# Two decoder layers with their gradients on one core: operand rows of dW in four row strips, and the first dW2 work moved ahead of the attention loop

## The chip, the cores and the metric

The kernel runs on one core of a Trainium2 chip. The metric is the device time in microseconds of one execution; the time before is the median of 7 runs. TensorE (PE) does matmuls and transposes, VectorE (DVE) and ScalarE (ACT) do everything that reads PSUM, GpSimd (POOL) issues the stores to HBM and SyncE (SP) the loads from HBM.

## The reference

Two layers, each an attention block and an MLP, share their weights. One token for each of two sequences passes through them, and the kernel returns the output and the gradients with respect to x, both caches, and all weights and biases.

```python
def _A_ref(x, k_cache, v_cache, wq, wo):       # x [2,1,1024], caches [2,4,16384,128]
    q = (x @ wq).reshape(B, Sq, 32, 128).transpose(0, 2, 1, 3)
    k, v = jnp.repeat(k_cache, 8, axis=1), jnp.repeat(v_cache, 8, axis=1)
    p = _softmax(jnp.einsum("bhqd,bhkd->bhqk", q, k) * Dh ** -0.5)
    o = jnp.einsum("bhqk,bhkd->bhqd", p, v)
    return o.transpose(0, 2, 1, 3).reshape(B, Sq, 4096) @ wo
def _B_ref(x, w1, b1, w2, b2):                  # w1 [1024,3584], w2 [3584,1024]
    h = _gelu(jnp.einsum("bsd,df->bsf", _layernorm(x), w1) + b1)
    return jnp.einsum("bsf,fd->bsd", h, w2) + b2
...
x = x + _A_ref(_layernorm(x), k, v, wq, wo); x = x + _B_ref(_layernorm(x), w1, b1, w2, b2)   # twice
_out, _vjp = jax.vjp(_f, x, k_cache, v_cache, wq, wo, w1, b1, w2, b2)
return (_out, *_vjp(grad_out))
```

The gradients of the caches (out_2, out_3) are 33.6 MB each. Those of the weights (out_4 for wq, out_5 for wo, out_6 for w1, out_8 for w2) are sums of four outer products each: two layers by two sequences.

## The kernel before, in words

Forward and backward passes run layer by layer; each streams the weights or the caches through SBUF in tiles of 128 x 4096 bf16 (1.05 MB). A pool `ld` has seven such buffers. One tile of K or V is a chunk of 4096 positions of one of eight groups (sequence x KV head); four chunks make a group. Four K and four V tiles of the last group (`keepK0` to `keepV3`) and one of each of another group (`keepxK`, `keepxV`) stay in SBUF from the earlier layer.

The change lies in the last stage, the backward pass of attention in layer 0, in which all big gradients are also written:

- **The wo stage.** `wob = Ahead(A_wo, ...)` loads wo in eight chunks of four rows. For each row `row(j)` turns the weights with eight transposes (`turn`, L313), and four iterations later `products(j)` multiplies them with the gradient (L340) into the PSUM tile `dops`. The last four rows are turned in iterations 28 to 31.
- **delta.** `do_delta` makes from `dops` the scaled gradient `doT_bf` and its dot product with the attention output, a chain of one matmul (`part_sum`) and some ten small DVE instructions that ends in `dlr`.
- **Operand rows.** The outer products need their operands as four rows (layer x sequence) on partitions. `rows_unit` (L949) transposes columns of `h_all`, `dh_all`, `o_all`, `dq_all` (into `rowsA`) and `gM_all`, `m_all`, `gA_all`, `n_all` (into `rowsB`); each pair of operands has one strip of 32 partitions of its own: strip 0 for dW2, 1 for dW1, 2 for dWo, 3 for dWq.
- **Units.** A unit of `dw_units` is one matmul of 4 rows by 128 x 512 (L1018) and its cast to bf16 in an SBUF tile, on ACT or DVE (`evac_cast`, L156 and L159; `pick` takes the engine with the smaller charged load). Eight units fill a tile of dW2 (seven of dW1), and `store` hands it to POOL's queue. Such a tile is called a home. Units wait in `fill`, those of dWq in `late`.
- **The opening.** The four kept chunks of the last group are done first: `scores` (L1194), a matmul with `dlr` (L1198), the product with the probabilities (L1202, `ds0`), the pairs `kv_pair` that make dV (L1159, eight matmuls and four casts for each half), and `dq_quad` (L411).
- **The loop.** Each step m turns two quarters of a V chunk (L1304), computes their scores, runs pairs for dK and dV, and calls `step_fill` for one unit (m < 4) or five.

All instructions stand in the order in which the Python code emits them, and each engine's queue runs in that order. Which SBUF tile a load or a home takes is also fixed when the program is written: two deques hold the free tiles, `by_read` (last read by an engine) and `by_store` (last given to a store). `new_home` takes from `by_read` first, `load_tile` from `by_store` first, `pump` issues loads while enough tiles are free. A load into a tile from `by_store` waits in SP's queue until that store has landed.

In PSUM there are two banks for transposes (`tp`), four for general use (`x`), one for accumulation and one small one (`sm`).

Of the kernel before, what the change touches and what calls it, by code (L numbers as in the profile page):

```python
# [23 lines left out]
def kernel(  # L24
# [50 lines left out]
    NLD = 7  # L75
    WIDE = 32
# [60 lines left out]
    def charge(eng, us):  # L137
        load[eng] += us
# [37 lines left out]
    def part_sum(src, n, name):  # L176
        ps = pm_([128, n], F32, name)
        PE.matmul(ps[:], lhsT=onesf[:], rhs=src, start=True, stop=True)
        return ps
# [520 lines left out]
    n_all = vec.tile([128, DJ, 4], BF16, name="n_all")  # L700
    o_all = vec.tile([128, HQ, 4], BF16, name="o_all")
    dq_all = vec.tile([128, HQ, 4], BF16, name="dq_all")
    gA_all = vec.tile([128, DJ, 4], BF16, name="gA_all")
    m_all = vec.tile([128, DJ, 4], BF16, name="m_all")
    h_all = vec.tile([128, FJ, 4], BF16, name="h_all")
    dh_all = vec.tile([128, FJ, 4], BF16, name="dh_all")
    gM_all = vec.tile([128, DJ, 4], BF16, name="gM_all")
# [86 lines left out]
    def attn_out_bwd(l, gT):  # L794
        V.tensor_copy(out=gA_all[:, :, lsl(l)], in_=gT[:])
        _, dops = w_pass(A_wo, HD, D, "do_ps", gT_bf=gA_all[:, :, lsl(l)])
        return do_delta(l, dops)

    def do_delta(l, dops):
# [5 lines left out]
        doT_bf = vec.tile([128, G, 8], BF16, name=f"doT_bf{l}")  # L805
        V.tensor_copy(out=doT_bf[:], in_=dof[:])
        prod = wrk.tile([128, G, 8], F32, name="dprod")
        V.tensor_tensor(out=prod[:], in0=dof[:], in1=sv["oT"][:], op=ALU.mult)
        dlp = part_sum(prod[:].rearrange("p g r -> p (g r)"), G * 8, "dl_ps")
        rest_ = wrk.tile([128, G * 8], F32, name="dl_rest")  # L810
        V.tensor_scalar(out=rest_[:], in0=dlp[:], scalar1=-1.0, scalar2=None, op0=ALU.mult)
# [12 lines left out]
        saved[f"a{l}"]["doT_bf"] = doT_bf  # L824
        return doT_bf
# [98 lines left out]
    for j in range(wob.J + 4):  # L924
        some(rest, 1)
        if j >= wob.J - 4 and j < wob.J:
            wob.row(j)
        if j >= 4:
            wob.products(j - 4, dops, gA_all[:, :, lsl(0)])
    TP = [pt([128, 8, 128], BF16, "tpm%d" % i) for i in range(2)]  # L930
    for t in TP:
        V.memset(t[:].bitcast(F32), 0.0)
    do_delta(0, pairs(dops, HQ))

    rowsA = ld.tile([128, LDW], BF16, name="rowsA", tag="ld")
    rowsB = wrk.tile([128, D], BF16, name="rowsB", tag="rowout")

    def rows_unit(srcs, dst, j0):  # L940

        def u():
            tp = mtp()
            n = 0
            for i, (colT, jlo) in srcs.items():
                jn = min(8, colT.shape[1] - jlo)
                n = max(n, jn)
                for j in range(jn):
                    PE.transpose(tp[32 * i:32 * i + 4, j, :], colT[:, jlo + j, :], ident[:], tile_position=(0, 32 * i))  # L949
            lo, hi = 32 * min(srcs), 32 * max(srcs) + 4  # L950
            evac_bf16(dst[lo:hi, j0 * 128:(j0 + n) * 128], tp[lo:hi, 0:n, :].rearrange("p a b -> p (a b)"), n * 128)

        return Unit(u)

    X = [px([128, 512], F32, "xm%d" % i) for i in range(4)]
    rot = {"x": 0, "tp": 0}


    by_read = deque(ld.tile([128, LDW], BF16, name="big", tag="ld") for _ in range(NLD - 1))
    by_store = deque()  # L960

    def nxt(what, lst):
        rot[what] += 1
        return lst[(rot[what] - 1) % len(lst)]

    def mx():
        return nxt("x", X)

    def mtp():
        return nxt("tp", TP)  # L970

# [13 lines left out]
    class Unit:  # L985
        def __init__(self, f, home=False):
            self.f, self.home = f, home

        def ready(self):
            return not self.home or n_free() > 3  # L990
# [4 lines left out]
    def dbias(rows, i, n, out_ap, name):  # L995
        p = 32 * i
        row = new_home()
        for c0 in range(0, n, 512):
            ps = mx()
            PE.matmul(ps[p:p + 1, :], lhsT=ones_bf[p:p + 4, 0:1], rhs=rows[p:p + 4, c0:c0 + 512], start=True, stop=True,  # L1000
                      tile_position=(p, p))
            evac_cast(row[p:p + 1, c0:c0 + 512], ps[p:p + 1, :], 512)
        store(out_ap.rearrange("(o f) -> o f", o=1), row[p:p + 1, 0:n], row)

    def dw_units(xrows, yrows, i, chunks, y0, ny, out_of):

        p = 32 * i
        box = {}
        units = []
        for j0, rb in chunks:  # L1010
            for j in range(rb):
                for c0 in range(0, ny, 512):
                    def u(j0=j0, rb=rb, j=j, c0=c0):
                        if j == 0 and c0 == 0:
                            box["t"] = new_home()
                        sv_ = box["t"][:, 0:rb * ny].rearrange("p (j n) -> p j n", j=rb)
                        ps = mx()
                        PE.matmul(ps[:], lhsT=xrows[p:p + 4, (j0 + j) * 128:(j0 + j + 1) * 128],  # L1018
                                  rhs=yrows[p:p + 4, y0 + c0:y0 + c0 + 512], start=True, stop=True, tile_position=(p, 0))
                        evac_cast(sv_[:, j, c0:c0 + 512], ps[:], 512)  # L1020
                        if j == rb - 1 and c0 + 512 >= ny:
                            store(out_of(j0, rb), sv_, box["t"])
                    units.append(Unit(u, j == 0 and c0 == 0))
        return units

    def rows_of(out_ap):
        return lambda j0, rb: out_ap[j0 * 128:(j0 + rb) * 128, :].rearrange("(j p) n -> p j n", p=128)

# [18 lines left out]
    def load_next():  # L1047
        job = jobs.popleft()
        t = loaded[job] = load_tile()
        open_loads.append(job)  # L1050
        if job[0] == "wq":
            src = wq_v[:, job[2]:job[2] + 4, job[1] * D:(job[1] + 1) * D]
            nc.sync.dma_start(t[:].rearrange("p (j n) -> p j n", j=4), src)
        else:
            src = (Kv if job[0] == "K" else Vv)[job[1], :, job[2] * TC:(job[2] + 1) * TC, :]
            nc.sync.dma_start(t[:].rearrange("p (t d) -> p t d", d=128), src)
# [14 lines left out]

    pump(NLD - 1, 0)

    fill = deque()
    fill.append(rows_unit({0: (gM_all, 0), 1: (m_all, 0), 2: (gA_all, 0), 3: (n_all, 0)}, rowsB, 0))
    for j0 in range(0, HQ, 8):
        srcs = {0: (h_all, j0), 1: (dh_all, j0), 2: (o_all, j0)}
        fill.append(rows_unit({i: v for i, v in srcs.items() if j0 < v[0].shape[1]}, rowsA, j0))
    units = [dw_units(rowsA, rowsB, 0, list(w_chunks(F, D)), 0, D, rows_of(out_8)),
            dw_units(rowsB, rowsA, 1, list(w_chunks(D, F)), 0, F, rows_of(out_6))]  # L1080
    while any(units):
        for u_ in units:
            if u_:
                fill.append(u_.pop(0))
    fill.append(Unit(lambda: dbias(rowsB, 0, D, out_9, "db2"), True))
    fill.append(Unit(lambda: dbias(rowsA, 1, F, out_7, "db1"), True))
    fill.extend(dw_units(rowsA, rowsB, 2, list(w_chunks(HD, D)), 0, D, rows_of(out_5)))
# [5 lines left out]
    for w in "VK":  # L1093
        cols[w] = vec.tile([128, G, 2, 8], BF16, name="cols" + w)
        for k in range(2):
            src = saved["a%d" % k]["qT_bf" if w == "K" else "doT_bf"]
            V.tensor_copy(out=cols[w][:, :, k, :], in_=src[:])
# [82 lines left out]
    def quarter(kv):  # L1180

        quarters[kv][1]()
        late_pe.append(quarters[kv][3])
        late.append(rows_unit({3: (dq_all, kv * 8)}, rowsA, kv * 8))
        late.extend(dw_units(rowsB, rowsA, 3, [(0, 4), (4, 4)], kv * D, D,
                             lambda j0, rb: dwq_v[:, j0:j0 + rb, kv * D:(kv + 1) * D]))
# [66 lines left out]

    open_dq(order[0])
    qs = [make_qm(w, order[0]) for w in "VK"]
    for c in range(NCH):
        dp = mx()[:].rearrange("p (q t) -> p q t", t=TC)
        for b in range(NB):
            scores(c, b, kept_vT(c)[:, b * 8:(b + 1) * 8, :], dp)
        ds0(c, dp)  # L1260
        if c > 0:
            by_read.append(held_tiles["V%d" % c])
        if c == 0:
            qs[0]()
            make_blks(0, None)
        elif c == 1:
            kv_pair("V", 0, 0)
            make_blks(1, None)
        elif c == 2:
            kv_pair("V", 0, 1)  # L1270
            qs[1]()
        else:
            kv_pair("V", 1, 0)
    for c in range(NCH):
        for q in range(2):
            dq_quad(c, q)
        if c == 1:
            kv_pair("V", 1, 1)
    accs[order[0]].evac()
    sch.later(0, accs[order[0]].reduce)  # L1280
    pump(NLD + 3, 4)

# [74 lines left out]
```

## Time and profile before

| | us |
|---|---|
| median of 7 runs | 1174.97 |
| lowest and highest | 1170.27 and 1176.93 |
| the profiled execution, device time | 1170.27 |
| its span | 1168.5 |
| PE busy in the span | 962.7 (82%) |
| DVE busy | 627.1 (54%) |
| ACT busy | 553.9 (47%) |
| DMA: moved 449.32 MB, mean | 385 GB/s |

The span is the time from the first to the last instruction that the profiler shows. "Busy" is the time in which an engine executes something; PE's weight loads (PEld) overlap its matmuls. The granted clock is the share of full speed at which PE ran. A row of the profile names the source line, the engine, the operation, the tile written and the tiles read, with partitions and elements.

### The profile page before, as it was taken

Reading aid. Unit: us, or ns where it says so; the run is one execution under the profiler, and the core shown is the slowest. Engines: PE = TensorE matmul, PEld = TensorE weight load, DVE = VectorE, ACT = ScalarE, POOL = GpSimd, SP = SyncE. Lnnn points to the kernel's source line nnn. Section 1 sums busy time; section 2 is a strip of 40 time slices with the busy share of each in tenths; the row PEclk is TensorE's granted clock in tenths of the full one; section 3 lists DMA queues with packets and bytes.
Section 4 is the critical chain, followed back from the end, with each engine's and each line's share of the span. In section 5 each row is a group of like instructions: output and inputs, shape, how many; then the busy total and the mean of one; then the engine's idle time right before and its main releaser. Section 6 shows DMA issues by size and latency. Waiting matters only on the chain. (4 is left out here: it accounts for less than half of the span.)

```text
span 1168.5 us, 40218 instructions
## 1 busy us (share of the span) xinstructions
PE 962.7 (82%) x17709; PEld 737.1 (63%) x17709; DVE 627.1 (54%) x1319; ACT 553.9 (47%) x1395; POOL 63.7 (5%) x113
## 2 busy tenths in 40 slices
PE   4888895487889875899997798888898988999886
PEld 3866673387767765888775598755554554555452
DVE  1544351133545433454835335568777877786784
ACT  0544351022535430344454433357767866685773
POOL 0000000000000000000000000001111111111111
PEclk9988795597989875999998899888778877786895
DMA  8999999998999989989999899667999999999996
GB/s 368 417 417 416 418 417 396 396 365 354 416 417 416 415 318 415 391 318 400 380 413 410 326 343 372 258 267 308 388 412 417 416 418 420 421 420 418 423 422 258
DMA packets 89131, 449.32 MB, mean 385 GB/s; under 512 B 7026, under 2 KB 7026, under 8 KB 49788
## 3 DMA queue, kind: packets, MB, share of 16 engines
q1 hardware_dynamic: 72204, 348.17, 74.8%
q0 software_dynamic: 16752, 98.59, 20.5%
q8 instruction: 138, 2.26, 0.8%
q14 instruction: 37, 0.30, 0.1%
HBM read 348.14 MB, written 98.58 MB: 382 GB/s over the span
## 5 line engine op out<-in xcount | busy, mean ns | idle before, releaser
L148 ACT COPY kT<-tp 128x512 int32<-128x512 int32 x204 | 119.7, 587 | 254.3 <-PE tp L379 246.4
L151 DVE COPY kT<-tp 128x1024 bf16<-128x1024 bf16 x164 | 112.0, 690 | 115.2 <-PE tp L379 105.3
L379 PE MATMUL tp<-ident,kv_K 128*128 128x128 bf16 x1728 | 146.1, 234 | 3.9 <-DMA kv_K<-in_A_k_cache_dram 3.9
L379 PEld LDWEIGHTS <-kv_K 128*128 128x128 bf16 x1728 | 111.0, 105 | 4.7 <-DMA kv_K<-in_A_k_cache_dram 4.5
L159 DVE CAST big<-xm 128x512 bf16<-128x512 f32 x141 | 91.7, 685 | 28.1 <-PE xm L1159 13.0
L156 ACT CAST big<-xm 128x512 bf16<-128x512 f32 x156 | 84.7, 593 | 20.0 <-PE xm L1018 10.8
L532 PEld LDWEIGHTS <-kT 128*128 128x128 bf16 x2048 | 76.6, 98 | 27.7 <-issue 21.8
L532 PE MATMUL sc<-qT_bf,kT 128*128 128x8 bf16 x2048 | 92.1, 171 | 0.5 <-issue 0.4
L379 PE MATMUL tp<-ident,kv_V 128*128 128x128 bf16 x864 | 72.4, 232 | 9.9 <-DMA kv_V<-in_A_v_cache_dram 8.9
L263 PE MATMUL wtp<-ident,wt 128*128 128x128 bf16 x928 | 75.2, 228 | 4.5 <-issue 3.2
L297 PEld LDWEIGHTS <-wt 128*128 128x128 bf16 x1696 | 48.9, 103 | 47.0 <-issue 14.9
L496 ACT ACTIVATE e_all<-sc,negm 128x64 bf16<-128x64 f32 x256 | 77.0, 345 | 1.0 <-DVE negm L491 1.0
L411 PE MATMUL acc_all<-kv_V,e_all 128*16 128x256 bf16 x864 | 46.3, 294 | 28.6 <-DMA kv_V<-in_A_v_cache_dram 15.4
L159 DVE CAST keepK<-xm 128x512 bf16<-128x512 f32 x92 | 59.9, 684 | 17.4 <-PE xm L1159 11.3
L148 ACT COPY wT<-wtp 128x512 int32<-128x512 int32 (+1 forms) x60 | 34.5, 575 | 70.1 <-PE wtp L263 61.7
L156 ACT CAST keepK<-xm 128x512 bf16<-128x512 f32 x105 | 56.2, 593 | 23.4 <-PE xm L1159 22.4
L151 DVE COPY wT<-wtp 128x1024 bf16<-128x1024 bf16 (+1 forms) x64 | 40.5, 636 | 49.4 <-PE wtp L263 45.8
L379 PEld LDWEIGHTS <-kv_V 128*128 128x128 bf16 x864 | 57.5, 104 | 11.8 <-DMA kv_V<-in_A_v_cache_dram 9.6
L156 ACT CAST keepV<-xm 128x512 bf16<-128x512 f32 (+1 forms) x98 | 53.4, 596 | 22.2 <-PE xm L1159 16.8
L263 PEld LDWEIGHTS <-wt 128*128 128x128 bf16 x928 | 57.4, 102 | 5.1 <-issue 3.7
L496 ACT ACTIVATION_READ_ACCUMULATOR e_all<-sc,negm 128x1 f32 x256 | 60.3, 236 | 0.0
L159 DVE CAST keepV<-xm 128x512 bf16<-128x512 f32 (+1 forms) x74 | 48.4, 685 | 20.5 <-PE xm L1159 15.8
(335 smaller groups left out, 1768.1 us busy)
## 6 DMA issues: line engine op xcount, KB each, us to landing
kv_K<-in_A_k_cache_dram SPq DMA_DIRECT2D x81, 1024.0 KB, 12.9
kv_V<-in_A_v_cache_dram SPq DMA_DIRECT2D x81, 1024.0 KB, 12.8
out_dram<-big POOLq DMA_DIRECT2D x36, 1024.0 KB, 17.8
wt<-in_A_wo_dram SPq DMA_DIRECT2D x32, 1024.0 KB, 11.0
wt<-in_B_w_dram SPq DMA_DIRECT2D x32, 896.0 KB, 14.4
out_dram<-keepK POOLq DMA_DIRECT2D x22, 1024.0 KB, 18.5
out_dram<-keepV POOLq DMA_DIRECT2D x18, 1024.0 KB, 18.3
wt<-in_A_wq_dram SPq DMA_DIRECT2D x16, 1024.0 KB, 9.2
```

The source lines that it names most:

```text
L148: S.copy(out=dst.bitcast(I32), in_=src.bitcast(I32))
L151: V.tensor_copy(out=dst, in_=src)
L156: S.copy(out=dst, in_=src)
L159: V.tensor_copy(out=dst, in_=src)
L263: PE.transpose(tp[:, o, :], wv[:, j, (o0 + o) * 128:(o0 + o + 1) * 128], ident[:])
L297: PE.matmul(fps[:, jo, :].rearrange("p (a b) -> p a b", b=2), lhsT=wv[:, j, jo * 128:(jo + 1) * 128], rhs=xT_bf[:, j0 + j, :].unsqueeze(1) ...
L379: PE.transpose(tp[:, j, :], cv[:, b * 8 + j, :], ident[:])
L411: PE.matmul(self.acc[cg:cg + 16, :], lhsT=coef(u), rhs=self.cv[:, t:t + 2, :].rearrange("p t d -> p (t d)"), start=False, stop=True, tile_ ...
L496: S.activation(out=e_all[:, g, f * half:(f + 1) * half, l, h, :], in_=sc[g][f][:, h, :].rearrange("p (a b) -> p a b", b=2), func=ACT.Exp, ...
L532: PE.matmul(sc[g][f][:, :, t % TH], lhsT=kT[:, j, :], rhs=q_bf[:, g, :], start=True, stop=True)
```

## The change

The operand rows get tiles of their own for each gradient: `R[0]` to `R[3]` are quarters of one `ld` tile, and `nr` and `dqr` serve dWq. Within each, the operand that varies from unit to unit is spread over all four strips of 32 partitions and the other one is repeated in all four, so that consecutive units use different strips. The transposes take 32 columns at a time (28 of them zeros or neighbours) and write a whole strip; the column tiles are seven columns longer so that this stays inside them.

The list of units begins with dW2 alone (it alternated between dW2 and dW1). The rows of gM and h and the first units are emitted inside the wo loop: two row units at j = 16, then four units at j = 19, 23, 27, 31 and 35. Three more follow in each of the opening's four chunks. Two `ld` tiles are homes from the start, and four loads instead of six are emitted ahead of the opening. In the opening the first two `make_blks` and the K side of `make_qm` come first, `do_delta` is cut in two (`do_scaled`, which writes straight into `cols["V"]`, and `delta`, which comes behind the scores of the first chunk), the scores of all four chunks use the one bank `sm`, and each V pair runs whole in its chunk.

```diff
+    def cols4(J, name):
+        t = vec.tile([128, J + 7, 4], BF16, name=name)
+        V.memset(t[:, (0 if name == "dq_all" else J):J + 7, :], 0.0)
...
     dops = px([128, 512], F32, "wob_b")
...
     class Unit:
+        spare = 0
...
-            return not self.home or n_free() > 3
+            return not self.home or n_free() > Unit.spare
...
+    def rows(name, dst, at, n, j0=0, slots=8):
+        tp = mtp()
+        flat = whole[name][:].rearrange("p j b -> p (j b)")
+        for k in range(slots):
+            for i in range(4):
+                j = at(i, k)
+                if j is not None and j < n:
+                    j += j0
+                    PE.transpose(tp[32 * i:32 * i + 32, k, :], flat[:, 4 * j:4 * j + 32], ident[:],
+                                 tile_position=(0, 32 * i))
...
+    def rows_rep(name, dst, j0=0):
+        rows(name, dst, lambda i, k: k, 8, j0)
+    def rows_split(name, dst, n):
+        rows(name, dst, lambda i, k: 4 * k + i, n, 0, n // 4)
...
+            todo = [(j, c) for c in range(ny // 512) for j in range(rb)]
...
+                    if split == "x":
+                        p, xo, yo = 32 * (jj % 4), jj // 4 * 128, c * 512
+                    else:
+                        p, xo, yo = 32 * (c % 4), jj * 128, c // 4 * 512
+                    PE.matmul(ps[:], lhsT=x[p:p + 4, xo:xo + 128], rhs=y[p:p + 4, yo:yo + 512], start=True, stop=True,
+                              tile_position=(p, 0))
...
+    R = ld.tile([128, LDW], BF16, name="rows", tag="ld")[:].rearrange("p (r n) -> r p n", r=4)
+    by_read.extend(ld.tile([128, LDW], BF16, name="home", tag="ld") for _ in range(NHOME))
+    fill.append(Unit(lambda: rows_rep("gM_all", R[0])))
+    fill.append(Unit(lambda: rows_split("h_all", R[1], FJ)))
+    fill.extend(dw_units(R[1], R[0], list(w_chunks(F, D)), D, rows_of(out_8), "x"))
...
     for j in range(wob.J + 4):
...
             wob.products(j - 4, dops, gA_all[:, :, lsl(0)])
-    TP = [pt([128, 8, 128], BF16, "tpm%d" % i) for i in range(2)]
-    for t in TP:
-        V.memset(t[:].bitcast(F32), 0.0)
-    do_delta(0, pairs(dops, HQ))
+        if j == 16:
+            feed(2)
+        if j > 16 and j % 4 == 3:
+            feed(4)
...
-    by_read = deque(ld.tile([128, LDW], BF16, name="big", tag="ld") for _ in range(NLD - 1))
...
-    pump(NLD - 1, 0)
+    for _ in range(NLD - 1 - NHOME):
+        load_next(ld.tile([128, LDW], BF16, name="big", tag="ld"))
...
+    rows_split("n_all", nr, DJ)
+    qk = make_qm("K", order[0])
+    make_blks(0, None)
+    qk()
+    make_blks(1, None)
+    prod = do_scaled(0, pairs(dops, HQ), cols["V"][:, :, 0, :])
     open_dq(order[0])
-    qs = [make_qm(w, order[0]) for w in "VK"]
+    qv = make_qm("V", order[0])
     for c in range(NCH):
-        dp = mx()[:].rearrange("p (q t) -> p q t", t=TC)
+        dp = pm_([128, 16, TC], F32, "dp")[:]
         for b in range(NB):
             scores(c, b, kept_vT(c)[:, b * 8:(b + 1) * 8, :], dp)
+        if c == 0:
+            qv()
+            delta(0, prod, mx())
+        kv_pair("V", c // 2, c % 2)
         ds0(c, dp)
         if c > 0:
             by_read.append(held_tiles["V%d" % c])
+            for q in range(2):
+                dq_quad(c - 1, q)
+        feed(3)
...
+    Unit.spare = 3
     pump(NLD + 3, 4)
```

## The prediction

> **What bounds the kernel now.** I read the page's slices first, for where the DMA engines fall short of full, then the window view by stage.
>
> ```profile
> DMA  8999999998999989989999899667999999999996
> GB/s 368 417 417 416 418 417 396 396 365 354 416 417 416 415 318 415 391 318 400 380 413 410 326 343 372 258 267 308 388 412 417 416 418 420 421 420 418 423 422 258
> ```
>
> A slice is 29.2 us. Slices 29 to 39 stand at 412 to 423 GB/s, nothing better is seen anywhere, and the three before 29 (730 to 818 us) are the deepest hole. The window view cut at the stages (columns: us, busy us of PE, PEld, DVE, ACT, POOL, granted clock, DMA share, GB/s):
>
> ```profile
> 738.50:749.30 10.80, 10.80 (x288) 10.54 (x287) 4.41 (x7) 3.93 (x7) 0.00 (x0) 1.00 1.05 398
> 749.30:769.90 20.60, 14.87 (x248) 8.23 (x246) 10.86 (x34) 6.51 (x13) 0.58 (x1) 0.59 0.48 192
> 769.90:815.00 45.10, 37.84 (x623) 25.91 (x619) 33.60 (x57) 31.90 (x62) 4.79 (x9) 0.92 0.81 319
> 815.00:1145.00 330.00, 290.97 (x3788) 172.26 (x3780) 251.94 (x427) 235.69 (x450) 49.20 (x83) 0.78 1.01 416
> 1145.00:1168.50 23.50, 13.76 (x108) 5.66 (x106) 10.27 (x23) 7.89 (x14) 3.14 (x5) 0.50 0.56 219
> ```
>
> Rows: last wo products, opening, head of the loop, loop, tail. From 815 to 1145 the 16 DMA engines are full, so only bytes count there: what was moved before 815 need not be moved after. In the wo stage PE is full (10.80 of 10.80) while DVE and ACT are under half busy; in the opening DMA runs at 0.48. Timeline of SP's queue:
>
> ```profile
> 738.56 3.15 SPq L1053 DMA_DIRECT2D big<-in_A_wq_dram  x2
> 744.12 1.15 SPq L1056 DMA_DIRECT2D big<-in_A_v_cache_dram  x2
> 745.73 0.33 SPq L1056 DMA_DIRECT2D big<-in_A_k_cache_dram  x1
> 748.47 0.33 SPq L1056 DMA_DIRECT2D big<-in_A_v_cache_dram  x1
> 768.64 0.33 SPq L1056 DMA_DIRECT2D keepV<-in_A_k_cache_dram  x1
> 776.21 0.33 SPq L1056 DMA_DIRECT2D keepV<-in_A_v_cache_dram  x1
> ```
>
> Six loads go out as wo tiles come free, then none for 20 us. The one at 768.64 writes the tile that POOL stores from 763.83. In the loop the longest waits of that queue are of the same kind:
>
> ```profile
> SPq L1056 <- DMA out_dram<-big: 105.6, 16, 16.7
> SPq L1056 <- DMA out_dram<-keepK: 61.8, 13, 12.1
> ```
>
> Loads wait for stores of the tiles they reuse: the loop is closed over the DMA. The end is paced by work, as PE's timeline there shows:
>
> ```profile
> 1144.19 1.01 PE L949 MATMUL tpm<-ident,dq_all 128*4 128x128 bf16 x8 [0.61 <-DVE dq_all L856]
> 1145.87 1.86 PE L1018 MATMUL xm<-rowsA,rowsB 4*128 4x512 bf16 x4 [0.67 <-ACT rowsA L148]
> ...
> 1152.72 5.27 PE L1018 MATMUL xm<-rowsA,rowsB 4*128 4x512 bf16 x12 [0.49 <-ACT keepK L156]
> ```
>
> **What the Trainium skill says.** "DMA: Bandwidth & Descriptors", Anatomy of one DMA, SWDGE path: about 2.0 us plus bytes/436e3 per DMA, so 4.4 us for 1.05 MB; here the lone store of 763.83 frees its tile at 768.64, 4.8 us. The same page, Queues, rings and completion order: the engines go round-robin between queue rows, so stores and loads halve each other; here the same store takes a median of 17.8 us over the run. "TensorEngine Tiling (Array Packing)", Key Properties and PSUM Bottleneck: tiles run in parallel, and evacuation then becomes the bottleneck. The trace agrees: two units in strips 0 and 1 start together (824.40 and 824.41), while the twelve of one strip in the tail take 5.27/12 = 0.44 us each at half clock, against a mean evacuation of (0.593+0.685)/4 = 0.32 us with both engines at work.
>
> **The change, part by part.**
>
> *Wo stage, added work.* feed(2) at j=16 puts 60 row transposes on PE. The 32 of L949 at 772.21 took 1.29 us, 40 ns each: 2.4 us, on the path since PE is full. Then five feeds of four units. dops holds one of the four x banks, so three matmuls go at once and the fourth waits in PE's queue for the first evacuation: 0.37 (L1018 at full clock) + 0.59 (ACT cast) + about 0.2 hand-over (the 0.21 before L1018 at 830), 1.2 us. Behind it wait the products, and behind those SP's loads. Part of the next group's wait is covered by 0.8 us of products. Walking the queue group by group I get the stage's end at 758.3 instead of 749.3: **+9.0 us** (bounds +5, if the products cover most waits, and +12). The turns of rows 28 to 31 share the evacuation queues; DVE and ACT have room (4.41 and 3.93 of 10.80).
>
> *Loads.* rows and two homes take the tiles of wo chunks 1, 2, 3, so four loads remain, the first after chunk 4's products: about 748.4, 750.4, 754.6, 757.0, not 738.6 to 748.5. DMA idles from 740 to 748, where it is full now. The first of these tiles is needed some 9 us into the loop (the held keepxV serves its first two steps): no stall.
>
> *Stores.* POOL's queue, empty here, gets dW2 chunks A (about 751), B (757), C and D (in the opening), each behind its last evacuation. These are 4 x 1.05 MB off the full stretch: 4.19/0.419 = **-10.0 us**.
>
> *Waits added.* Unit 17 reuses A's home: ACT's cast waits for A's landing, with the next K and V casts behind it; A shares with loads, so 2.1 MB at 0.419 (5.0 us) and the lone store's overhead (4.8 - 0.5 issue - 2.5 transfer = 1.8) after 751.3, landed at 758 against 757.4 wanted: 0.6 us. The first V pair takes B's home: landed about 764.3, wanted 764.5: nothing, by a hair. Bounds 0 to +8.
>
> *Opening.* It loses both memsets (1.0 us) and takes delta (750.6 to 753.3) off the front, behind scores and V pair; cols V is written directly. It gains the 8 n transposes, 12 units (12 x 0.32 = 3.8 us of both evacuators, DVE and ACT being 10.86 and 6.51 of 20.6), and one dp bank instead of four: scores of chunk c+1 now wait for chunk c's L1202. A chunk then costs 1.0 (scores) + 0.5 (pair) + 0.6 (hot) + 1.3 (pair casts ahead on DVE) + 0.7 (L1202) = about 3.5 us; today the middle ones are 3.3 to 3.8 apart. Net **+0.5 us**, bounds -4 and +5. So the loop starts about 779.4 instead of 769.9.
>
> *Head of the loop.* Four loads less at its start, but four stores more are out. Load by load against the stores that they wait for, I count twelve loads out 40 us into the loop in both. Five fill slots that carried row units (L949 in 772 to 795) now carry units: 5 x 131 KB = 0.66 MB earlier, **-1.6 us** (0 to -2.5). m, dh, gA and o rows move into the full stretch: 124 transposes x 40 ns = 5 us of PE's 39 idle us there, at nothing; were PE the limit, +5.
>
> *Strips in the loop.* At nothing: DMA is the limit. If not, a gain of up to 0.1 us x 144 units is out of reach, since the casts take their 0.32 anyway.
>
> *Tail.* dq rows are 32 transposes instead of 8: 24 x 0.13 (1.01/8) is +3.1 serial, +0.3 if the four column groups overlap; I take +1.0. The sixteen units become bound by casts: (1.86+5.27) - 16 x 0.32 = -2.0, of which the four ahead of L847 may hide a little: -1.9. Sum **-0.9**, bounds -2 and +2.
>
> **Sum.** 9.0 + 0.5 - 10.0 - 1.6 - 0.9 = **-3.0 us**. The profiled execution took 1170.27 (span 1168.5 + 1.8): 1167.3. That one was the fastest of seven, 4.7 below the median; on the median, 1174.97 - 3.0 = **1172.0**. A measurement of this kernel tells about 0.3%, 3.5 us, from no change.
>
> **Rivals.**
> - *A, the homes block the casts (slower).* Place: ACT's queue, unit 17 and the first V pair. If store B needs not 7 but 12 us or more, as the loop's 17.8 suggests, then ACT and soon DVE stand still 5 us at the pair and some at unit 17; the loop starts at 785 to 790. Price +5 to +12 over the likeliest, 1177 to 1184. It decides once B lands later than some 3.5 us after the pair wants it. For it: two loads are in flight with each store. Against it: the DMA is otherwise idle there.
> - *B, the groups hide (faster).* DVE and ACT have 2 x 10.8 - 4.41 - 3.93 = 13.3 us free in the wo stage, and twenty casts take 12.8; if feeds cost only 0.6 us and the opening shrinks by its delta chain, the loop starts near 774: -8 to -11, about 1165. Against it: PE's order is fixed and it was full.
> - *C, the end is no longer DMA-bound.* Fill runs out some 45 us before it does now (1110). A step of pairs alone takes 20/4.6 = 4.35 us at full clock (1110 to 1130) against 2.1 MB = 5.0 us of DMA; at a granted 0.75 it would be 5.8, and DMA idles 0.8 x 10 steps: +8, 1180. For it: the mean clock of 0.78 in the loop. Against it: those 20 us had 1.00.
> - *The strips don't overlap:* +0.22 us x 15 in the wo stage, +3; inside the range.
>
> **How the numbers follow.** Likeliest 0.50 (own range 1167 to 1179: faster 0.22, same 0.20, slower 0.08), A 0.23 (slower 0.20, same 0.03), B 0.15 (faster), C 0.12 (slower 0.10, same 0.02). Sum: faster 0.37, same 0.25, slower 0.38: a near balance of delay against bytes, with the most likely point just below zero. The range 1159 to 1188 takes in A, B and C but their ends.
>
> **What would show it.** Right: four dW2 stores on POOL before the loop; the wo stage ends near 758, the loop's first keepxV transposes near 779; DMA share 0.7 or more in the opening; DMA full from about 820; fill gone near 1065. Wrong: a cast of home waiting for DMA out_dram for microseconds (A); the loop starting before 775 (B); GB/s below 400 after 1065 (C); a loop start past 783 with no such wait means the opening's chunks were costed too low.

## The result: slower by 0.7%

| | us |
|---|---|
| after, median of 14 runs (1176.5 to 1189.6) | 1184.6 |
| before, median of the 35 runs beside it | 1174.95 |
| ratio after / before, 95% interval | 1.0071 [1.0053, 1.0088] |
| span of the profiled execution, after | 1181.0 |
| span of the profiled execution, before | 1168.5 |

By the ratio the change costs 8.3 us (6.2 to 10.3), by the medians 9.7. The spans lie 12.5 us apart because the profile of before happens to be its fastest execution; a second profile of the same kernel has a span of 1172.7. Below, profiles tell where, and the ratios tell how much; the stretches of single executions scatter by some us, before the changed part too (the two profiles of before end the wo stage at 749.35 and 752.78).

The slices of the page of after:

```profile
DMA  9999999998999989989999897779999999999985
GB/s 371 418 419 419 420 419 395 396 345 365 418 420 416 413 327 416 392 311 414 397 413 406 313 329 271 242 253 365 381 413 422 423 415 418 421 412 422 423 370 218
```

The loop is as full as before (412 to 423 GB/s), but the slice of 370 ahead of the last one is new: the end has less to move and takes its time all the same. The window view, at the cuts of the prediction:

```profile
738.50:749.30 10.80, 9.26 (x239) 7.52 (x237) 5.73 (x9) 5.17 (x10) 0.00 (x0) 0.96 0.25 81
749.30:769.90 20.60, 14.05 (x198) 8.99 (x195) 10.10 (x32) 6.24 (x12) 1.59 (x2) 0.58 0.88 302
769.90:815.00 45.10, 40.05 (x505) 23.22 (x505) 28.31 (x47) 28.79 (x56) 4.77 (x8) 0.63 0.85 315
815.00:1145.00 330.00, 282.57 (x4055) 174.21 (x4055) 246.39 (x419) 233.00 (x445) 46.66 (x80) 0.79 1.00 410
1145.00:1181.00 36.00, 20.10 (x214) 9.22 (x214) 18.74 (x40) 14.98 (x28) 4.74 (x8) 0.54 0.60 238
```

The first two rows have changed places: 81 GB/s instead of 398 at the end of the wo stage, 302 instead of 192 after it. What the stores move early, the loads had moved there before. SP's queue shows the loads, POOL's the stores:

```profile
747.51 2.90 SPq L1098 DMA_DIRECT2D big<-in_A_wq_dram  x2
755.99 2.71 SPq L1101 DMA_DIRECT2D big<-in_A_v_cache_dram  x2
779.56 0.33 SPq L1101 DMA_DIRECT2D home<-in_A_k_cache_dram  x1
```

```profile
750.33 0.82 POOL L963 DMA_DIRECT2D out_dram<-home  x1 [45.21 <-DVE home L160]
758.30 0.77 POOL L963 DMA_DIRECT2D out_dram<-home  x1 [7.15 <-ACT home L157]
775.21 0.55 POOL L963 DMA_DIRECT2D out_dram<-home  x1 [16.14 <-DVE home L160]
776.19 0.75 POOL L963 DMA_DIRECT2D out_dram<-home  x1 [0.43 <-DVE keepV L160]
```

Stores A and B go out at 750.33 and 758.30, as forecast (751 and 757); then POOL stands for 16.14 us. The reason is on ACT and DVE (in brackets the idle time before, and what ended it):

```profile
759.94 0.58 ACT L157 CAST home<-xe 128x512 bf16<-128x512 f32 x1 [1.94 <-DMA out_dram<-home]
769.53 3.03 ACT L157 CAST home<-xm 128x512 bf16<-128x512 f32 x6 [5.66 <-DMA out_dram<-home]
```

```profile
759.96 1.29 DVE L160 CAST home<-xe 128x512 bf16<-128x512 f32 x2 [2.40 <-DMA out_dram<-home]
```

Unit 17 waits for store A to land, the first V pair for store B. B lands about 769.5, 11.2 us after its issue; the two V loads of 755.99 were in flight with it. They did not share the DMA by halves: the DMA view of the window 759.10 to 763.50 (packets, MB, share) has loads (q1) moving and the store (q0) hardly at all.

```profile
q1 hardware_dynamic: 165, 1.18, 88.1%
q0 software_dynamic: 3, 0.01, 0.5%
```

After the landing no transfer is left in flight: in the window 770 to 775 the DMA moves 3 GB/s.

PE's timeline of the wo stage (start, duration):

```profile
741.65 0.63 PE L987 MATMUL tpe<-ident,gM_all 128*32 128x128 bf16 x32
742.31 0.57 PE L987 MATMUL tpe<-ident,h_all 128*32 128x128 bf16 x28
...
746.16 0.37 PE L1022 MATMUL xe<-rows 4*128 4x512 bf16 x1 [0.71 <-ACT home L157]
...
757.31 0.97 PE L341 MATMUL wob_b<-gA_all,wt 128*128 128x32 bf16 x32
758.22 0.39 PE L1022 MATMUL xe<-rows 4*128 4x512 bf16 x3
760.70 0.58 PE L1022 MATMUL xe<-rows 4*128 4x512 bf16 x1 [2.10 <-DVE home L160]
...
770.17 1.56 PE L1022 MATMUL xm<-rows 4*128 4x512 bf16 x3 [1.35 <-ACT home L157]
```

In four of the five groups the last matmul waits 0.7 to 0.8 us for an evacuation. The last products end at 757.31 + 0.97 = 758.28; the fifth group, that of j = 35, stands behind them and ends at 761.28, after a wait of 2.10 us (store A). At 770.17 PE waits again, with the units of the first chunk, behind the casts that waited for store B. The loop's first step (keepxV transposes, L1341) starts at 784.25, against 769.87 before. The head has become 14.4 us longer.

What it bought is seen with the trace cut at the loop's first transpose and at the `dlr` matmul of the last chunk, before first:

```profile
738.50:769.87 31.37, 25.64 (x532) 18.74 (x532) 15.28 (x40) 10.43 (x20) 0.58 (x1) 0.73 0.68 263
769.87:1128.79 358.92, 317.86 (x4286) 192.61 (x4283) 274.01 (x463) 257.56 (x494) 51.86 (x88) 0.81 0.99 404
1128.79:1168.50 39.71, 24.75 (x230) 11.25 (x225) 21.80 (x44) 17.93 (x33) 5.27 (x9) 0.58 0.74 301
```

and after:

```profile
738.50:784.25 45.75, 37.26 (x630) 22.47 (x627) 23.56 (x52) 20.80 (x40) 3.44 (x5) 0.65 0.63 219
784.25:1142.25 358.00, 306.37 (x4330) 190.18 (x4327) 264.22 (x449) 249.78 (x477) 49.05 (x84) 0.78 1.01 408
1142.25:1181.00 38.75, 22.41 (x254) 10.51 (x249) 21.49 (x44) 17.60 (x33) 5.27 (x9) 0.57 0.59 232
```

Time by rate gives the bytes: 8.3, 145.0 and 12.0 MB before, 10.0, 146.1 and 9.0 MB after. Three of the four stores of units land in the head (775.21 is a V pair's, the fourth goes out at 784.75), but two loads fewer do, so the head is ahead by 1.7 MB and not by 4.2. The loop carries no less than before. What is missing is missing in the tail, where the rate falls from 301 to 232 GB/s and the time by 1.0 us: bytes do not bound that stretch. The loop takes 358.0 instead of 358.9 us.

### The profile page after: what moved, and what is told of

Read it like the earlier page. It is cut to its first block, busy times and chain, and to the rows that moved or that the text cites. A ratio compares the mean times of both kernels' runs of the same rounds, so it can differ in the third digit from the quotient of the medians.

```text
span 1181.0 us, 40584 instructions
## 1 busy us (share of the span) xinstructions
PE 963.7 (82%) x17877; PEld 738.9 (63%) x17877; DVE 625.2 (53%) x1325; ACT 556.1 (47%) x1397; POOL 63.8 (5%) x113
## 5 line engine op out<-in xcount | busy, mean ns | idle before, releaser
L157 ACT CAST keepV<-xm 128x512 bf16<-128x512 f32 x112 | 60.8, 593 | 31.7 <-PE xm L1191 23.4
L412 PE MATMUL acc_all<-kv_V,e_all 128*16 128x256 bf16 x864 | 47.5, 301 | 28.2 <-DMA kv_V<-in_A_v_cache_dram 15.6
L160 DVE CAST keepV<-xm 128x512 bf16<-128x512 f32 x85 | 55.1, 684 | 19.6 <-PE xm L1191 11.1
L160 DVE CAST keepK<-xm 128x512 bf16<-128x512 f32 x84 | 54.4, 685 | 20.7 <-PE xm L1191 16.8
L157 ACT CAST keepK<-xm 128x512 bf16<-128x512 f32 x94 | 50.6, 591 | 16.6 <-PE xm L1191 13.3
L160 DVE CAST big<-xm 128x512 bf16<-128x512 f32 x77 | 49.7, 684 | 14.2 <-PE xm L1191 8.7
L1022 PE MATMUL xm<-rows 4*128 4x512 bf16 x156 | 42.9, 419 | 16.4 <-ACT home L157 2.4
## 6 DMA issues: line engine op xcount, KB each, us to landing
out_dram<-big POOLq DMA_DIRECT2D x18, 1024.0 KB, 16.8
```

The lines of the kernel that those rows point to most:

```text
L157: S.copy(out=dst, in_=src)
L160: V.tensor_copy(out=dst, in_=src)
L412: PE.matmul(self.acc[cg:cg + 16, :], lhsT=coef(u), rhs=self.cv[:, t:t + 2, :].rearrange("p t d -> p (t d)"), start=False, stop=True, tile_ ...
L1022: PE.matmul(ps[:], lhsT=x[p:p + 4, xo:xo + 128], rhs=y[p:p + 4, yo:yo + 512], start=True, stop=True, tile_position=(p, 0))
```

## The experiments

Theory after the result: a later start of the loop is paid in full, 32 units less return only a part of 10 us, and the rest of the change (divided delta, strips) gains something that the prediction put at nothing. Rivals: the landing waits alone turned a gain into a loss; the new layout itself costs; the lag is absorbed by the loop. Unless said otherwise diffs are against the kernel after. The opening's length is counted here from the end of the last wo products to L1341; the expectations count from the start of that group of products, 1.0 to 1.3 us more. For e6 it is counted from the end of the added transposes. "Clock" is the granted clock of the opening. The runs of before beside these kernels had medians from 1174.95 to 1176.1, so the ratios compare better than the medians do; e5 and e11 have four runs each.

| kernel | median us | ratio to before | opening | clock | loop | span |
|---|---|---|---|---|---|---|
| before | 1174.95 | 1 | 20.5 | 0.58 | 358.9 | 1168.5 |
| after | 1184.6 | 1.0071 [1.0053, 1.0088] | 26.0 | 0.51 | 358.0 | 1181.0 |
| e1, no early units, six loads | 1168.24 | 0.993 [0.9907, 0.9953] | 15.9 | 0.78 | 361.3 | 1168.1 |
| e3, no early units, four loads, two homes | 1169.92 | 0.9937 [0.9917, 0.9958] | 17.8 | 0.62 | 361.8 | 1164.4 |
| e9, opening alone | 1168.94 | 0.9959 [0.9941, 0.9976] | 16.8 | 0.80 | 363.9 | 1169.3 |
| e8, strips alone | 1171.38 | 0.9967 [0.995, 0.9983] | 19.8 | 0.77 | 357.5 | 1166.7 |
| e7, e1 with alternated units | 1171.47 | 0.9959 [0.9945, 0.9974] | 16.3 | 0.79 | 361.3 | 1163.8 |
| e2, 16 units early | 1178.9 | 1.0022 [1.0004, 1.0041] | 18.1 | 0.53 | 362.1 | 1173.9 |
| e4, 25 units early, no landing wait | 1178.73 | 1.0018 [1.0001, 1.0036] | 20.5 | 0.50 | 357.4 | 1177.3 |
| e10, 12 units in the opening | 1172.13 | 0.9968 [0.9955, 0.9982] | 19.1 | 0.82 | 362.4 | 1169.7 |
| e6, e3 with a delay | 1179.89 | 1.0036 [1.0023, 1.005] | 17.2 | 0.70 | 363.0 | 1175.2 |
| e5, e3 less 32 units | 1164.32 | 0.991 [0.9879, 0.9941] | 17.0 | 0.80 | 355.9 | 1161.2 |
| e11, e3 less 112 units | 1154.61 | 0.9821 [0.9775, 0.9866] | 17.9 | 0.62 | 346.8 | 1151.7 |

The kernel before, profiled a second time (e0), took 1174.52 us: opening 20.0, loop 360.1, span 1172.7.

> The kernel before, profiled once more: its first profile came from its fastest execution (1170.3, median near 1175). If the gain of the strips (8 us) is in the loop, this profile shows chunk 28 of the loop some 5 us later than 1103.5, at one or several places between chunk 4 and chunk 28, and the same tail of 39 to 40 us. If the gain is in the opening, the loop's first chunk is later instead.

It is a typical run; against it the loop of after starts 11.5 us later and its span is 8.3 us longer. The 3.4 us by which it lags the first profile at the end of the wo stage lie ahead of everything that the expectation asked about.

**Without the early units (e1, e3).** e1 also has no homes and V pairs in their old places:

```diff
-    NHOME = 2
+    NHOME = 0
...
-        if j == 16:
-            feed(2)
-        if j > 16 and j % 4 == 3:
-            feed(4)
...
-        feed(3)
```

e3 takes away the feeds alone.

> Strips and the two-part delta alone: no units ahead of the loop, no homes, six loads ahead as before, V pairs in their old places. Late start (the loop of the changed kernel starts at 784.3 instead of 769.9 because of the units' work and of two waits for stores to land): the loop starts near 770, the time is 1173 to 1176 (before: 1175), a us gained in the tail. Fewer loads ahead as the cause: 1175 too. Rows and strips themselves as the cause (320 row transposes for 152, dW2 no longer in turn with dW1): 1179 to 1184.

> The changed kernel with no units and no row units ahead of the loop, but with its four loads ahead and its two homes. Late start: the loop starts near 769, 1174 to 1177. Fewer loads ahead: V and K loads stay behind through the loop, 1181 to 1184. Rows and strips: 1179 to 1184, and the first kernel of this group the same.

Both beat before by 0.6 to 0.7%, more than any of the expectations allowed. e3 differs from after by the feeds alone: the early units cost 0.0134 of 1175, 16 us, and all the rest of the change gains 7 to 8 us. Two loads less, the two homes and the earlier V pairs together make no difference between e1 and e3 that these runs can tell.

**Where the gain comes from (e8, e9, e7).** e8 is e1 with the opening of before:

```diff
+    for t in TP:
+        V.memset(t[:].bitcast(F32), 0.0)
+    delta(0, do_scaled(0, pairs(dops, HQ), doT0[:]))
...
-        dp = pm_([128, 16, TC], F32, "dp")[:]
+        dp = mx()[:].rearrange("p (q t) -> p q t", t=TC)
```

e9 is the kernel before with the new opening, V pairs placed as in e1; its diff against before:

```diff
-    do_delta(0, pairs(dops, HQ))
...
+    qk = make_qm("K", order[0])
+    make_blks(0, None)
+    qk()
+    make_blks(1, None)
+    prod = do_scaled(0, pairs(dops, HQ), cols["V"][:, :, 0, :])
...
+        if c == 0:
+            qv()
+            delta(0, prod, mx())
```

> No early units, the new operand rows in four strips, but the opening as before: memsets and the undivided delta behind the wo stage, one x bank for the scores of each chunk, V pairs in their old places. Theory (the gain of the version without early units comes for the larger part from the divided delta): from the last wo products to the loop it took 17.2 us there against 21.8 before, and a later loop is paid in full, so this kernel loses 4 to 5 us of that gain: opening 21 to 22 us, ratio 0.996 to 0.998, some 3 us below before by the strips in the loop and the tail. Rival (the strips carry all of it): ratio 0.993 as without early units. Rival of the prediction (strips at nothing but the tail's 0.9 us): ratio 0.999.

> The kernel before with the new opening alone: delta in two parts, the K side of make_qm and two make_blks ahead of it, scores in the one small bank; operand rows, units, their order and the six loads as before, and the two memsets stay behind the wo stage. Theory: the opening shortens by about 3.5 to 4.5 us (17.2 us plus up to 1.0 for the memsets against 21.8), all of it arrives at the end: ratio 0.996 to 0.997. Rival (the loop is bound by its bytes and gives the start back): ratio 1.000. Rival (the opening carries the whole gain): 0.993.

The two halves, 3.9 us (strips) and 4.8 us (opening), add up to e1's 8.2 within the intervals. The opening's half can be read from PE. Before:

```profile
748.04 1.31 PE L340 MATMUL wob_b<-gA_all,wt 128*128 128x32 bf16 x40
750.61 0.43 PE L178 MATMUL dl_ps<-dprod,onesf 128*128 128x64 f32 x2 [1.26 <-DVE dprod L808]
753.40 0.28 PE L1102 MATMUL tpm<-ident,colsV 128*16 128x128 bf16 x1 [2.36 <-DVE colsV L1097]
...
753.78 1.03 PE L1194 MATMUL xm<-colsV,keepV 128*128 128x16 bf16 x32
```

and in e9:

```profile
750.68 0.40 PE L1136 MATMUL tpm<-ident,e_all 128*128 128x128 bf16 x4
751.70 0.22 PE L1104 MATMUL tpm<-ident,colsV 128*16 128x128 bf16 x1 [0.61 <-DVE colsV L808]
751.85 0.97 PE L1196 MATMUL dp<-colsV,keepV 128*128 128x16 bf16 x32
752.75 0.28 PE L1112 MATMUL xm<-r16sb,sel 16*128 16x128 bf16 x2
752.96 0.43 PE L178 MATMUL xm<-dprod,onesf 128*128 128x64 f32 x2
755.58 0.58 PE L1200 MATMUL dp<-dlr,hot 128*128 128x512 bf16 x1 [2.19 <-DVE dlr L825]
```

In both PE waits for the chain of delta (2.36, 2.19), but in e9 scores, blocks and Qm are done ahead of it, while before they all stand behind. A part of the 3.7 us between the two openings is the clock (0.58 and 0.80): e3 and e5 have the same opening, and it took 17.8 us at 0.62 and 17.0 at 0.80. In e9's own profile the loop is 5.0 us longer than before (3.8 against e0), so that profile does not show the gain arriving at the end; the 4.8 us rest on the runs. The same leaning is in all six profiles with the new opening, no units in the wo stage and nothing left out (loop 361.3 to 363.9; with the old opening 357.5 to 360.1), so the loop may give back a part of an earlier start. Why was not tested.

e7 is e1 with units of dW2 and dW1 in turn, as before:

```diff
+    while any(two):
+        for q_ in two:
+            if q_:
+                fill.append(q_.pop(0))
```

> The strips alone (e1) with the units of dW2 and dW1 in turn, as before, instead of dW2 first. If the strips' parallel matmuls carry e1's gain: 1167 to 1170, as e1. If it was the order of the gradients (one open home instead of two): 1174 to 1177.

1171.5 lies between e1 and before, and the intervals of e7 and e1 overlap: whether the order of the units carries a part of the strips' 3.9 us stays open. About 1.4 us of it is in the tail (from the last `dlr` matmul to the end 38.3 us in e8, 39.7 before and in e9).

**Waits or delay (e4, e2).** e4 feeds 16 units in the wo stage and nine in the last three chunks of the opening, so that no cast finds its home's store in flight:

```diff
-        if j > 16 and j % 4 == 3:
+        if 16 < j < 35 and j % 4 == 3:
...
-        feed(3)
+        if c > 0:
+            feed(3)
```

e2 keeps the first of these edits and has no `feed(3)` at all.

> The changed kernel without the feed at j = 35 and without the feed in the opening's first chunk: 25 units ahead instead of 32, the V pair in the first home (landed), the third dW2 tile in keepV1. No cast waits for a store. If the two waits are the whole loss: loop start near 777 and 1174 to 1177. Late start by work as well: start near 780, 1177 to 1180. Fewer loads ahead: 1183.

> The changed kernel with only sixteen units ahead (the feeds at j = 19, 23, 27, 31), none at j = 35 and none in the opening; the V pair then takes a home whose store has long landed. Late start: both landing waits go (2.4 us at unit 17, 5.7 us of ACT at the pair) and twelve units leave the opening; the loop starts at 774 to 777, 16 units taken from the loop give back some 5 us: 1175 to 1178. Fewer loads ahead: as the changed kernel, 1183. Rows and strips: 1181 or more.

Without the waits and with seven units less e4 is 0.0053 (6.2 us) below after, so the waits and those units have a price; the waits alone are some 3.5 us of it on PE (below). But e4 does not get below before, nor does e2 with half the units. The rival "waits alone" falls. e2 has the sixteen units of the wo stage only, and that stage is 9.1 us longer by its profile; the run is 0.0085 (10 us) above e3.

**Is a later start paid in full (e6)?** Against e3:

```diff
+    idle = mtp()
+    for k in range(160):
+        PE.transpose(idle[:, k % 8, :], ident[:], ident[:])
```

> The kernel without early units (e3) with 160 more transposes of a constant behind the wo products: a delay of the opening and the loop of [...]8.5 us (to 11 at a lower clock), nothing else. A late start is paid in full: 1178 to 1181. The loop takes it up (its loads land during the delay): 1170 to 1174.

The transposes took 9.09 us and the loop starts 9.45 us later; the run costs 0.0099, 11.6 us more than e3 (about 8 to 16 by the two intervals), and the loop is not shorter (363.0 and 361.8). No part of the delay is seen to be absorbed.

**What bytes return (e5, e11, e10).** Against e3, e5 leaves out the first 32 units, e11 all 112 of dW2 and dW1:

```diff
-    fill.extend(dw_units(R[1], R[0], list(w_chunks(F, D)), D, rows_of(out_8), "x"))
+    fill.extend(dw_units(R[1], R[0], list(w_chunks(F, D))[4:], D, rows_of(out_8), "x"))
```

> The kernel without early units (e3) with the first 32 units of dW2 left out altogether: four tiles of out_8 are not computed and not stored. It gives the return on moving these units without the price. Bytes count (the prediction): 4.19 MB less, 10 us less, 1160. The end of the loop hides them (stores that are late only run into the tail, where the DMA has room): 1166 to 1170.

> The version without early units (two homes, four loads), and none of the 112 units of dW2 and dW1 are computed or stored: all tiles of out_8 and out_6 are left out, 14.68 MB. Question: what the loop's time consists of when units go. Rival of the prediction (the loop is bound by its bytes at 0.419 MB/us): 35 us faster than 1169.9, so 1135, ratio 0.966. Theory (the return is proportional, as with 32 units: 3.2 to 5.6 us): 11 to 20 us faster, ratio 0.978 to 0.985, with fill gone some 40 us earlier against the loop's start. Third possibility (the first units removed return something, later ones nothing, because pairs and loads alone set the pace once the fill is gone): 5 to 8 us faster, ratio about 0.988, DMA well below 412 GB/s in the last third and PE waiting there for loads.

4.19 MB less gave 0.0027 by the ratios (3.2 us; by the two intervals anything from nothing to 9) or 5.6 by the medians, instead of 10; 14.68 MB less gave 0.0116 (13.6 us, 6 to 21) or 15.3, instead of 35. That is 0.10 to 0.18 us for a unit of 131 KB, a third to a little over a half of its time at 0.419 MB/us.

The traces show where the rest stays. Cut each loop 60 us after its start, where the DMA has become full, and at the landing of the fifth cache load from the end, the last landing that the traces record. Before and after:

```profile
829.87:1109.34 279.47, 249.04 (x3152) 146.17 (x3149) 211.58 (x359) 198.13 (x379) 42.57 (x71) 0.77 1.01 417
1109.34:1168.50 59.16, 42.31 (x547) 23.67 (x547) 37.86 (x72) 33.02 (x63) 7.40 (x13) 0.72 0.83 341
844.25:1122.82 278.57, 236.78 (x3318) 144.45 (x3318) 204.89 (x350) 193.57 (x368) 38.48 (x66) 0.78 1.02 419
1122.82:1181.00 58.18, 39.81 (x571) 22.88 (x571) 37.19 (x72) 32.37 (x62) 7.40 (x13) 0.72 0.72 292
```

e3 and e11:

```profile
824.55:1105.57 281.02, 249.98 (x3375) 150.14 (x3371) 215.02 (x364) 201.49 (x386) 41.58 (x70) 0.77 1.01 416
1105.57:1164.40 58.83, 41.67 (x571) 24.02 (x571) 37.37 (x72) 32.65 (x63) 7.40 (x13) 0.69 0.82 334
826.45:1090.40 263.95, 214.36 (x3196) 135.28 (x3193) 182.26 (x315) 171.05 (x326) 32.90 (x56) 0.77 1.01 419
1090.40:1151.70 61.30, 42.87 (x631) 24.88 (x627) 41.23 (x78) 35.62 (x69) 7.94 (x14) 0.74 0.64 255
```

The first row of each pair runs at 413 to 419 GB/s in all fourteen profiles, e11 too: there the time follows the bytes. e11 moves 6.3 MB less than e3 in it and takes 17.1 us less. The second row takes 57.6 to 61.3 us in all fourteen, whatever it moves (20.2 MB before, 17.0 after, 15.6 in e11): there missing bytes shorten nothing. Nor do they in the first 60 us of the loop: e11 moves 18.1 MB there and e3 22.3, but e11 is no further on (its fifth `dlr` matmul of the loop comes 73 us after the start, that of e3 after 66). Of the 14.68 MB of e11 only 6.3 left the stretch that pays for them, and of the early units of after none did: it moves 116.7 MB in the middle stretch, before 116.5. When that fifth load from the end lands, the stores of after are 2.7 MB further on (84.0 MB since 738.5, against 81.3). So later stores moved up into the room, and the loads did not come sooner; that each load waits for the store of the tile it reuses fits this, but no run takes that rule away.

That the transfers set the pace near the end of this stretch is seen on PE too. In after the last unit of `fill` is done at 1052 and the last of dWq ahead of the tail at 1093; then PE waits for loads, longer than anywhere in the loop before (3.5):

```profile
1109.87 0.60 PE L412 MATMUL acc_all<-big,dX 128*16 128x256 bf16 x8 [5.38 <-DMA big<-in_A_k_cache_dram]
1114.05 1.04 PE L1341 MATMUL tpm<-ident,big 128*128 128x128 bf16 x8 [3.58 <-DMA big<-in_A_v_cache_dram]
```

e10 has twelve units where they disturb least:

```diff
-        feed(3)
+        feed(2 if c == 0 else 4)
```

(the feeds of the wo stage are gone, as in e3).

> The version with two homes and four loads, no units in the wo stage, but two row units in the opening's first chunk and four units in each of the other three: twelve units (1.57 MB, one tile stored) where the DMA has room and no store is waited for. Theory (a later loop is paid in full, bytes brought forward return a little over 1 us for a tile): the opening grows by some 5 us (row units 1.2, three groups of four casts about 1.3 each), the return is about 1.5 to 2 us: 3 us slower than without, ratio 0.996 to 0.998. Rival of the prediction (bytes off the full stretch count 1 us for 0.419 MB): 3.7 us back for the bytes, ratio about 0.994 to 0.995. If the groups hide beside waits of the opening: below 0.993.

Twelve units lengthen the opening by 1.3 us (19.1 against e3's 17.8) or 2.1 (against 17.0 in e5, the same opening at a nearer clock), not by the 5 expected; four of them behind `dq_quad` take PE 0.63 to 1.05 us. The run is still 0.0031 above e3, with intervals that just touch: the bytes brought forward returned nothing that shows. Of the versions that leave nothing out e1 and e3 have the lowest ratios; both beat before and after.

## Why the prediction was wrong

It gave 1172.0 with a balance near zero; measured is a loss of 8.3 us. Step by step (profiles of after and before; in brackets against e0). The wo stage is counted from the products ahead of the first feed (741.65 before, 741.37 after), so that what lies ahead of the change drops out:

| step | predicted | measured |
|---|---|---|
| wo stage with its five groups, landing wait taken off | +9.0 | +10.8 |
| opening with its units, landing wait taken off | +0.5 | +0.4 (+0.9) |
| landing waits | +0.6, left out of the sum | +3.5 (1.4 at unit 17, 2.1 at the V pair) |
| loop: four stores early, five slots, strips | -11.6 | -0.9 (-2.1) |
| tail | -0.9 | -1.0 (-1.1) |

The measured column sums to 12.8 (12.0); the runs say 8.3 (6.2 to 10.3), so single profiles give these sizes to a few us only. The largest miss is the loop's row by far, the second the landing waits.

- **The step that failed: "Stores", -10.0, with the -1.6 of the fill slots.** It says that from 815 to 1145 "only bytes count there: what was moved before 815 need not be moved after". The first half holds up to the fifth load from the end: with 6.3 MB less e11 takes 17.1 us less there. The second half failed: after moves 116.7 MB in that stretch and before 116.5, in 278.6 and 279.5 us. In the head stores took the place of loads (1.7 MB ahead instead of 4.2), and what was ahead was missing only at the end, 17.0 MB instead of 20.2, in 58.2 and 59.2 us. The prediction's stretch reached to 1145, past that last landing at 1109: the DMA is still full there, but the time no longer follows the bytes.
- **Landing waits, 0.6 + 0: rival A was right about the waits.** The 0.6 is not in the prediction's sum. The forecast had B land 7 us after its issue; it took 11.2, near the 12 at which rival A begins. Unit 17's group waits 2.10 us instead of 0.7, which is 1.4; from the first chunk's `dlr` matmul to the next scores PE takes 3.43 us in after and 1.37 in e4, which is 2.1. What was wrong is how a store lands among loads. The Trainium skill ("DMA: Bandwidth & Descriptors", Queues, rings and completion order) says that each engine takes turns between the queues it has work for; that they halve each other was the prediction's own reading, and this trace does not show turns for the first 5 us (the store 0.01 MB against 1.18 from 759.10 to 763.50). The 17.8 us median of the run, quoted beside it, was the warning. A's price (1177 to 1184) nearly reaches the result, but by itself A does not explain it: e4 has no such wait and is not below before.
- **The wo stage was right in kind**: the fourth matmul of a group waits for the first evacuation. It came 1.8 us above +9.0, inside the bounds. The 758.3 counted all five groups; at 758.28 only four were done, and the fifth ended at 761.28. The row transposes took 1.2 us where 2.4 were written, the groups more.
- **"Opening +0.5" was right as a net, "strips: at nothing" too pessimistic.** The new opening without units is 2.7 to 4.6 us shorter (e3, e9, e1; the clock has a part in it), because scores and blocks no longer stand behind the chain of delta; units then use that up. The strips without early units gain 3.9 us (e8; 2.0 to 5.9), some 1.4 of them in the tail.
- **The tail was right in sum** (-0.9 and -1.0), with some luck: its two terms, +1.0 for the rows and -1.9 for the units, came to nothing and -2.4 on PE. Its rows:

```profile
1157.64 1.05 PE L987 MATMUL tpm<-ident,dq_all 128*32 128x128 bf16 x32 [0.61 <-DVE dq_all L869]
1159.37 0.62 PE L1022 MATMUL xm<-dqr,nr 4*128 4x512 bf16 x4 [0.69 <-ACT dqr L149]
...
1165.77 4.11 PE L1022 MATMUL xm<-dqr,nr 4*128 4x512 bf16 x12 [0.49 <-ACT keepV L157]
```

32 transposes take what 8 took before (1.05 and 1.01), four units 0.62 instead of 1.86 and twelve 4.11 instead of 5.27.

- **Rival C** is excluded: `fill` was gone at 1052, but the DMA moves 421 GB/s from there to 1122, and the loop as a whole is 0.9 us shorter, not 8 longer. **Rival B** is excluded by the loop's start. A slip of reading changed nothing: slices 29 to 38, not 39, stand at 412 to 423 GB/s; the last is at 258. Of the signs of being wrong named beforehand, "a cast of home waiting for DMA out_dram for microseconds" was the one that appeared.

## What to carry to other kernels

Before crediting bytes that are moved earlier, follow them to the stretch from which they vanish. Here the time of the loop's middle, where the DMA was full, did follow its bytes, but the same bytes still passed through it, and the missing ones came off an end whose length does not follow its bytes. A delay of 9 us ahead of this loop was paid in full as far as the runs can tell (e6), so work may be put ahead of such a loop only where an engine waits and no buffer of the loads is taken, and even there e10 shows no gain. And when a change has several parts, price each as if it were alone: here the two parts that seemed free were a gain of 0.7%, and the headline part lost twice that.

## What the runs showed of the hardware

- Transposes of 32 columns whose results go in turn to four groups of 32 output partitions took about 20 ns each at full clock (32 in 0.63 us at 741.65) and 33 ns at half clock (32 in 1.05 us). With one group of 4 columns at a time, 8 in 1.01 us at half clock, it was 126 ns.
- Four matmuls of 4 rows in four different strips take 0.62 us at half clock, against 1.86 us in one strip; twelve take 4.11 us, 0.34 each, while ACT and DVE evacuate for 3.66 and 3.92 us of 4.20.
- A store of 1.05 MB with two loads of the same size in flight took 11.2 us to land, against 4.8 us for the lone one of before. Its first packets moved 5.1 us after the issue (those of store A, also with loads beside it, after 4.9), those of the lone store after 1.2.
- With loads and stores both waiting, the DMA moved 413 to 419 GB/s over stretches of 264 to 283 us in all fourteen profiles.
